# A fused attention and feed-forward kernel: first block's records cut short, output weights loaded and clamped apart, tables from the counts' low words, a new written order

## The chip, the cores and the metric

The kernel runs on one core of a Trainium2 chip. The metric is the device time in microseconds of one execution. Three runs of the kernel before gave 719.63, 720.25 and 720.26 us; their median is 720.25.

## The reference

Attention with a local window, a few global keys and a bias that grows with distance, on q, k, v of 4 batches, 8 heads, 768 positions and 64 columns, all float32; n_local is 96 and n_global is 8. Then a gated feed-forward layer on the 3072 tokens of 512 columns, with 1536 inner columns, whose weights are float64 in the input.

```python
scores = scale * q @ k.T + bias            # bias = -slope_h * distance
scores = where(is_global | is_local, scores, -1e9)
a = softmax(scores)                        # is_local: 0 <= rel < n_local
x = (a @ v) as 3072 x 512
out = (sigmoid(x @ w_gate) * (x @ w_val)) @ w_out
```

## The kernel before

**Blocks.** The tokens are worked in seven blocks: blocks 0 to 3 are three tiles of 128 positions, blocks 4 to 6 four tiles. For each block the attention of four pairs of heads gives x, in a high and a low part (`xh`, `xl`). Then twelve feed-forward steps f, one for each 128 inner columns, multiply x with the gate and value weights of f (`half_in`, L775 for block 0's first step and L787 for the others, into `ps_g` and `ps_u`) and the product with the output weights of f (`ff_out`, L859, into `ps_o`). The gate matmuls of f are three for each of four slices: low weights by high x, high weights by low x, high by high.

**Weights.** The weights come as float64. The kernel makes float32 from them by integer work on the halves of the words, once for each f (twelve blocks; `weights[f]` is 128 x 1536 float64: 1024 columns for gate and value, 512 of output weights). `conv_load` (L176) loads all 1536 columns into one tile `raw` (two buffers). Then come pieces, each one instruction, named by a letter: `B` and `b` (ACT, L194 and L198) take bits of the low words for the 1024 and the 512 columns; `N` and `P` (DVE, L218 and L223) clamp the high half-words in two steps into `neg`; `A` and `a` (DVE, L234 and L236) add them; `H` (ACT, L249) makes the high part `w1h` and `L` (DVE, L182) the low part `w1l`. For f in 2, 4, 6, 8, 10 the clamps of the 1024 columns are done on ACT instead (`Q`, `R`, L209 and L214, and `D` on DVE), and `N` and `P` take the 512 columns only. For the other seven `N` and `P` take 1536 columns.

**The order.** Two strings of words, OPENING and WALK, set the order of every engine's instructions up to the end of block 0: `hold` chains each instruction to the one before on its engine (PE, DVE, ACT, POOL and SP, the queue that issues the DMAs). In OPENING, `S01` is the scores of pair 0, tile 1 (PE, L436), `D01` their reduction with the bias table to a minimum (DVE, L453), `E01` the exponentials with their sums (ACT, L473), `T01` the transposes (PE, L490), `C01` their copy (DVE L499 or ACT L501), `I0` adds and inverts the sums (L506, L508), `R0` spreads the inverses (PE, L516) and `J0` copies them (ACT, L528), `V0` multiplies with the values (PE, L727), `X0` scales, `H0` and `L0` split x, `F0` begins block 0's first feed-forward step, `q`, `v` and `w` load a pair's record, its values and a weight block, `z` and `t` make the bias tables, `k3` is three filler matmuls on zeros (L111), and `c1N` is piece N of weight block 1. In WALK, `G2`, `U2` and `O2` are the gate, value and output matmuls of step 2, `P2` the gate's function (ACT, L798), which frees `ps_g`, `M2` the product (DVE, L807), and `S`, `D`, `E`, `N`, `T`, `C`, `V` the attention of block 1 (L561, L569, L583, L605, L618, L623, L727). From block 1's feed-forward on, a table and a scheduler set the order.

**Records.** `qk` holds for each block and pair the queries, two counts (n_local and n_global as 64-bit words) and the keys by slots: 96 old positions, then for each tile 8 global and 128 own positions, 892 columns in all. The first record is loaded in three transfers, whose first brings the counts, the first tile's queries and its keys. Tile 0 of block 0 uses neither old nor global positions. The counts go through two instructions (L98, L99: low word and sign, then both words) to `nf`, from which the tables and a later check of their range are made.

Of the kernel before, what the change touches and what calls it, by code (L numbers as in the profile page):

```python
# [19 lines left out]
P = 128  # L20
TB = 3
# [11 lines left out]
def attn_moe_kernel(ctx, tc, qT, kT, v, qk, vv, qk4, vv4, weights, out, B, H, S, D):  # L33
# [58 lines left out]
    Q0 = QW - P  # L92
    both = wraw.tile([P, QKW], F32, name="qk", bufs=QB)
# [27 lines left out]
    def build_tables():  # L121

        nl, ng = nf[:, 0:1], nf[:, 1:2]
# [68 lines left out]
    def piece_bits(c):  # L192
        c["bits"] = bits = wraw.tile([P, NW1], I32, name="bits")
        ins = nc.scalar.activation(bits, c["low"][:, 0:NW1], AF.Copy, scale=2.0 ** -13)  # L194
        hold("ACT", behind(ins, last_exp))

    def piece_bits2(c):
        ins = nc.scalar.activation(w2f[c["f"]], c["low"][:, NW1:], AF.Copy, scale=2.0 ** -13)  # L198
        hold("ACT", behind(ins, last_exp))

    def neg_of(c):
        if "neg" not in c:
            c["neg"] = wraw.tile([P, NW], I16, name="neg")
        return c["neg"], NW1 if c["relu"] else 0

    def piece_relu_neg(c):
        if c["relu"]:
            neg, a = neg_of(c)
            hold("ACT", nc.scalar.activation(neg[:, :a], c["high"][:, :a], AF.Relu, scale=-8.0, bias=-8.0 * 14336.0))  # L209

    def piece_relu_top(c):
        if c["relu"]:
            c["top"] = top = wraw.tile([P, NW1], I16, name="top")
            hold("ACT", nc.scalar.activation(top, c["high"][:, :NW1], AF.Relu, scale=8.0, bias=-8.0 * 14336.0))  # L214

# [35 lines left out]
    def piece_low(c):  # L251
# [6 lines left out]
        L=piece_low, Q=piece_relu_neg, R=piece_relu_top,  # L258
    )

    def pieces(j, names):
# [3 lines left out]
        if "loaded" not in c:  # L265
            conv_load(j)
# [53 lines left out]
    def load_step(bi, s):  # L320
# [4 lines left out]
        if bi == 0 and s > 1:  # L325
            qr, kr = (w2f[NF - 1 - 2 * (s - 2) - j].bitcast(F32) for j in range(2))
            hold("SP", nc.sync.dma_start(kr[:, 0:KW], qk[i, :, QW:]))
# [984 lines left out]
```

## Time and profile before

| what | value |
|---|---|
| median of 3 runs | 720.25 us |
| the profiled execution | 720.3 us |
| its span, first to last instruction | 718.5 us |
| PE busy in the span | 709.9 us |
| DVE, ACT, POOL busy | 462.1, 404.4, 180.5 us |
| TensorE's granted clock | 1.0 of full speed throughout |

The span is what the views of the trace cover; 1.8 us of the execution lie around it. A busy time counts an instruction from its start to its modelled end, so PE's busy time holds matmuls that overlap. The first 32 us hold block 0's attention (the opening), and up to about 112 us lie block 0's feed-forward and block 1's attention (the walk).

### The profile page before, as it was taken

How to read it: one execution, taken by the hardware profiler on the slowest of the kernel's cores; microseconds unless marked ns; L12 is line 12 of the kernel's file. 1: busy time of each engine (PE TensorE's matmuls, PEld its weight loads, DVE VectorE, ACT ScalarE, POOL GpSimd, SP SyncE). 2: the span in 40 equal slices, each digit the busy share in tenths (PEclk: the TensorE clock that was granted, in tenths of full speed). 3: DMA queues.
4: the chain of work that ended last, by engine and by line, in shares of the span. 5: the costliest groups of instructions: out<-in, count | busy, mean ns of one | idle time of the engine just before them, and what ended most of it. 6: DMA issues, size and time to landing. Idle time of an engine off the chain costs nothing.

```text
span 718.5 us, 11830 instructions
## 1 busy us (share of the span) xinstructions
PE 709.9 (99%) x4102; PEld 613.0 (85%) x4102; DVE 462.1 (64%) x1237; ACT 404.4 (56%) x956; POOL 180.5 (25%) x177
## 2 busy tenths in 40 slices
PE   8999999999999999999999999999999999999997
PEld 6777789899999999999998888888888888888885
DVE  7989885578867855676876876667677583111112
ACT  7987886565656645665665655455655453322222
POOL 7200012323323322333232223232222121112111
PEclk9999999999999999999999999999999999999999
DMA  8856632635435442353625423324724311100001
GB/s 331 310 204 246 235 110 66 147 62 130 90 89 123 97 95 59 89 136 78 142 64 146 116 69 86 89 56 81 188 58 92 96 39 30 59 0 1 0 1 61
DMA packets 106815, 74.95 MB, mean 104 GB/s; under 512 B 73984, under 2 KB 96896, under 8 KB 105216
## 3 DMA queue, kind: packets, MB, share of 16 engines
q1 hardware_dynamic: 106752, 74.16, 38.6%
q8 instruction: 33, 0.54, 0.3%
q14 instruction: 30, 0.25, 0.1%
HBM read 50.54 MB, written 6.29 MB: 79 GB/s over the span
## 4 chain that ended last, share of the span: by engine, by line
PE 89%; DVE 5%; DMA 2%; ACT 2%; issue 1%; SPq 0%; DVEq 0%
PE ps_u L787 26%; PE ps_g L787 26%; PE ps_o L859 22%; PE ps_s L651 4%; PE ps_t L859 3%; DMA raw<-in_weights 2%; PE ps_v L727 2%; PE ps_s L727 1%; PE ps_t L727 1%; DVE neg L218 1%; DVE neg L223 1%; PE ps_o L890 1%; PE ps_v L561 1%; DVE work L453 1%; PE ps_t L618 1%
## 5 line engine op out<-in xcount | busy, mean ns | idle before, releaser
L182 POOL TENSOR_TENSOR w2l<-w2f,w2h 128x512 fp32r<-128x512 f32 x76 | 103.4, 1360 | 331.4 <-ACT w2h L273 319.2
L787 PE MATMUL ps_g<-xh,w1l 128*128 128x384 f32 (+1 forms) x332 | 121.3, 365 | 0.3 <-ACT work L798 0.2
L787 PE MATMUL ps_u<-xh,w1l 128*128 128x384 f32 (+1 forms) x332 | 120.4, 363 | 0.4 <-DVE work L807 0.4
L787 PE MATMUL ps_g<-xh,w1h 128*128 128x384 f32 (+1 forms) x332 | 119.3, 359 | 0.0
L787 PE MATMUL ps_g<-xl,w1h 128*128 128x384 f32 (+1 forms) x332 | 119.2, 359 | 0.0
L787 PE MATMUL ps_u<-xh,w1h 128*128 128x384 f32 (+1 forms) x332 | 119.2, 359 | 0.0
L787 PE MATMUL ps_u<-xl,w1h 128*128 128x384 f32 (+1 forms) x332 | 119.1, 359 | 0.0
L182 POOL TENSOR_TENSOR qs<-hh,qs 128x256 fp32r<-128x256 f32 x72 | 58.4, 812 | 182.6 <-ACT qs L373 182.2
L807 DVE SCALAR_TENSOR_TENSOR work<-work,ps_u 128x384 f32<-128x384 f32 (+1 forms) x77 | 47.0, 610 | 81.5 <-PE ps_u L787 79.1
L859 PE MATMUL ps_o<-w2l,hh 128*128 128x512 f32 x225 | 88.6, 394 | 0.0
L859 PE MATMUL ps_o<-w2h,hh 128*128 128x512 f32 x225 | 87.7, 390 | 0.0
L583 ACT ACTIVATE work<-work,nms 128x232 f32<-128x232 f32 (+1 forms) x168 | 78.1, 467 | 11.7 <-DVE nms L569 11.6
L859 PE MATMUL ps_o<-w2h,hl 128*128 128x512 f32 x225 | 84.1, 391 | 0.0
L818 ACT ACTIVATE hh<-work 128x384 fp32r<-128x384 f32 (+1 forms) x77 | 43.9, 570 | 63.1 <-DVE work L807 61.1
L182 DVE TENSOR_TENSOR hl<-work,hh 128x384 fp32r<-128x384 f32 (+1 forms) x76 | 50.3, 662 | 40.9 <-PE ps_t L859 27.2
L373 ACT ACTIVATE qs<-hh 128x256 fp32r<-128x256 f32 x72 | 30.0, 417 | 79.4 <-issue 52.5
L569 DVE CUSTOM_DVE_ANT_0 work<-ps_s,tab 128x232 f32<-128x232 f32 x132 | 47.8, 395 | 39.7 <-PE ps_s L651 39.0
L787 PEld LDWEIGHTS ps_g<-xh,w1l 128*128 128x128 f32 x332 | 62.4, 188 | 8.9 <-issue 1.5
L787 PEld LDWEIGHTS ps_u<-xh,w1l 128*128 128x128 f32 x332 | 62.4, 188 | 8.2 <-DVE work L807 0.9
L273 ACT ACTIVATE w2h<-w2f 128x512 fp32r<-128x512 f32 x76 | 47.7, 627 | 38.2 <-PE ps_t L859 21.7
L798 ACT ACTIVATE work<-ps_g 128x384 f32<-128x384 f32 (+1 forms) x84 | 44.2, 526 | 43.7 <-PE ps_g L787 42.6
L787 PEld LDWEIGHTS ps_g<-xl,w1h 128*128 128x128 f32 x332 | 62.5, 188 | 6.6 <-issue 0.2
(193 smaller groups left out, 1288.0 us busy)
## 6 DMA issues: line engine op xcount, KB each, us to landing
raw<-in_weights SPq DMA_DIRECT2D x12, 1536.0 KB, 6.6
vp<-in_vv SPq DMA_DIRECT2D x28, 384.0 KB, 4.1
hh<-in_qk SPq DMA_DIRECT2D x144, 64.0 KB, 2.4
out<-ost SPq DMA_DIRECT2D x21, 256.0 KB, 3.1
kr<-in_qk SPq DMA_DIRECT2D x8, 320.0 KB, 3.2
qk<-in_qk SPq DMA_DIRECT2D x5, 446.0 KB, 7.3
kr<-in_qk SPq DMA_DIRECT2D x8, 252.0 KB, 2.7
hl<-in_vv SPq DMA_DIRECT2D x12, 128.0 KB, 3.1
```

Source lines behind the costliest of these rows:

```text
L182: return eng.tensor_tensor(out, a, b, op=ALU.subtract)
L273: ins = hold("ACT", nc.scalar.activation(hi, w, AF.Copy))
L373: ins = hold("ACT", nc.scalar.activation(qs[:, :, 0], qr, AF.Copy))
L569: ins = nc.vector.tensor_tensor_reduce(sb[:, j, :w], ps[:, :w], (tabs0 if zero else tabs)[2 * s + j], -SCALE, 3.0e38, op0=ALU.add, op1=ALU ...
L583: ins = nc.scalar.activation(sb[:, j, :w], sb[:, j, :w], AF.Exp, scale=-1.0, bias=nm, accum_out=sm[:, j:j + 1])
L651: ins = nc.tensor.matmul(ps[j][:, :w], qs[:, j, hl], st["ks"][:, j, k0:k0 + w], start=(hl == 1), stop=(hl == 0),)
L727: ins = nc.tensor.matmul(av[j * D:(j + 1) * D, t * P:(t + 1) * P], vt[t][:k, j * D:(j + 1) * D], st["pT"][t][:k, m * j + c], start=(c == 0 ...
L787: ins = nc.tensor.matmul(ps[:, :n], wt[f][:, i, c], xt[c], start=(k == 0), stop=(k == 3 * NC - 1))
L798: last_gate[:] = [hold("ACT", nc.scalar.activation(a[:, :n], ps[:, :n], AF.Tanh, scale=0.5))]
L807: hold("DVE", nc.vector.scalar_tensor_tensor(h[:, :n], a[:, :n], 1.0, ps[:, :n], op0=ALU.add, op1=ALU.mult))
L818: hold("ACT", nc.scalar.activation(hh[:, :n], a[:, :n], AF.Copy))
L859: ins = nc.tensor.matmul(outs[bi][t], ht[:, t * P:(t + 1) * P], wt, start=(f == 0 and k == 0), stop=(f == NF - 1 and k == len(parts) - 1),)
```

## The change

Four things are done. The first block's records (`qk0`, a new input) leave out the 104 columns of old and global keys that tile 0 never reads, 788 columns for 892, and its first 128 columns of values stay behind. The first record comes in two transfers, 260 and 528 columns, and the counts stand at its front. The output weights of a block are loaded apart (`o`, tile `rawo`, two buffers, 512 columns of float64, 512 KB) and clamped apart (`n`, `p`, tile `neg2`), so `N` and `P` are 1024 columns wide for seven blocks and gone for five, while `n` and `p` are 512 wide for all twelve. The tables are made from the counts' low words, one copy (`near`); the two instructions that give `nf` come later in the order (word `n`). The strings OPENING and WALK are written anew, with two fillers (`k2`) for three.

```diff
-    for part in (slice(Q0 - CNT, QW + WIN), slice(0, Q0 - CNT), slice(QW + WIN, QKW)):
-        hold("SP", nc.sync.dma_start(both[:, part], qk[0, :, part]))
-    words = both[:, Q0 - CNT:Q0].bitcast(I32).rearrange("p (w h) -> p w h", h=2)
-    wf = cpool.tile([P, 2], F32, name="wf")
-    nc.vector.scalar_tensor_tensor(wf, words[:, :, 0], 0.0, words[:, :, 1], op0=ALU.is_lt, op1=ALU.add)
-    nc.vector.scalar_tensor_tensor(nf, wf, 2.0 ** 32, words[:, :, 0], op0=ALU.mult, op1=ALU.add)
+    for part in (slice(0, CNT + 2 * P), slice(CNT + 2 * P, QK0)):
+        hold("SP", nc.sync.dma_start(both[:, part], qk0[0, :, part]))
+    words = both[:, 0:CNT].bitcast(I32).rearrange("p (w h) -> p w h", h=2)
+    near = cpool.tile([P, 2], F32, name="near")
+    nc.vector.tensor_copy(near, words[:, :, 0])
+
+    def counts():
+        wf = cpool.tile([P, 2], F32, name="wf")
+        hold("DVE", nc.vector.scalar_tensor_tensor(wf, words[:, :, 0], 0.0, words[:, :, 1], op0=ALU.is_lt, op1=ALU.add))
+        hold("DVE", nc.vector.scalar_tensor_tensor(nf, wf, 2.0 ** 32, words[:, :, 0], op0=ALU.mult, op1=ALU.add))
...
-        nl, ng = nf[:, 0:1], nf[:, 1:2]
+        nl, ng = near[:, 0:1], near[:, 1:2]
...
-        raw = wraw.tile([P, 4 * NW + 4], I16, name="raw", bufs=2)
-        hold("SP", nc.sync.dma_start(raw[:, 1:1 + 4 * NW], weights[j].bitcast(I16)))
+        c["low"], c["high"] = load_part(j, "raw", 0, NW1)
...
+    def conv_load2(j):
+        c["low2"], c["high2"] = load_part(j, "rawo", NW1, NW)
...
+    def load_part(j, name, a, b):
+        n = b - a
+        raw = wraw.tile([P, 4 * n + 4], I16, name=name, bufs=2)
+        hold("SP", nc.sync.dma_start(raw[:, 1:1 + 4 * n], weights[j, :, a:b].bitcast(I16)))
...
     def piece_neg(c):
-        neg, a = neg_of(c)
-        ins = nc.vector.tensor_scalar(neg[:, a:], c["high"][:, a:], -18432.0, -14336.0, op0=ALU.max, op1=ALU.min)
-        hold("DVE", behind(ins, last_min))
+        if not c["relu"]:
+            c["neg"] = wraw.tile([P, NW1], I16, name="neg")
+            clamp_low(c["neg"], c["high"])
...
+    def piece_neg2(c):
+        c["neg2"] = wraw.tile([P, DM], I16, name="neg2")
+        clamp_low(c["neg2"], c["high2"])
+
+    def piece_top2(c):
+        clamp_high(c["neg2"], c["high2"])
...
-        hold("SP", nc.sync.dma_start(vp.rearrange("p t c x -> p (t c x)"), vv[bi * NPAIR + s]))
+        cols = slice(P if bi == 0 else 0, TB * 2 * P)
+        hold("SP", nc.sync.dma_start(vp.rearrange("p t c x -> p (t c x)")[:, cols], vv[bi * NPAIR + s, :, cols]))
...
     OPENING = (
-        "S00 q1 z2 k3 D00 z3 S01 z1 E00 S02 D01 E01 T00 S10 S11 D02 t1 w0 T01 E02 v0 T02 t3 S12 C00 D10 "
+        "z2 z1 S00 k2 q1 D00 S01 S02 S10 E00 t1 w0 D01 D02 D10 n t2 E01 o0 T00 E02 S11 S12 v0 t3 C00 T01 I0 "
...
     WALK = (
-        "c2R P0 c2b q1 q0 S0 c2N w3 c2B D0 c2Q E0 G1 c2P M0 c2a c2D P1 c2A v1 N0 v0 S1 U1 D1 O0 c2H E1 M1 "
+        "c2R q0 c2n c2b o3 P0 c2Q c2B M0 c2p S0 D0 G1 E0 c2a w3 c2D c2A q1 o4 N0 S1 c2H D1 c3n U1 c3N c3p E1 "
...
```

How the order moves is shown at three places. The first is ACT in the opening, from the exponentials of pair 0 on (L473 before, L500 in the change: exponentials; L501 and L528: copies of the transposes; L198 and L214: the conversion of the output weights' low words; L528 and L555: the copy of the inverses). Before:

```order
L473 ACTIVATE work,sums<-work,nms 128x232 x4
L501 COPY pT<-ps_o_242 128x512
L198 ACTIVATE w2f_154<-raw 128x512
L501 COPY pT<-ps_t 128x512
L473 ACTIVATE work,sums<-work,nms 128x128 x2
L473 ACTIVATE work,sums<-work,nms 128x232 x4
L528 COPY hl<-ps_o_280 128x384
L473 ACTIVATE work,sums<-work,nms 128x128 x2
```

In the change:

```order
L500 ACTIVATE work,sums<-work,nms 128x232 x4
L500 ACTIVATE work,sums<-work,nms 128x128 x2
L528 COPY pT<-ps_o_259 128x512
L528 COPY pT<-ps_t 128x512
L500 ACTIVATE work,sums<-work,nms 128x232 x2
L555 COPY hl<-ps_o_283 128x384
L214 ACTIVATE w2f_152<-rawo 128x512
L500 ACTIVATE work,sums<-work,nms 128x232 x2
```

The conversion that reads the loaded output weights stood between the two copies of pair 0's transposes; it now stands behind both copies, four exponentials and the copy of the inverses.

The second is SP in the walk (L176 and L193: weights; L334 and L360: records of block 1; L392 and L419: values). Before, from the third weight block on:

```order
L176 DMA raw<-in_weights 128x6144
L334 DMA qk<-in_qk 128x892 x2
L176 DMA raw<-in_weights 128x6144
L392 DMA vp<-in_vv 128x768 x2
L176 DMA raw<-in_weights 128x6144 x4
L334 DMA qk<-in_qk 128x892
L176 DMA raw<-in_weights 128x6144 x2
```

In the change, from the same block's gate weights on:

```order
L193 DMA raw<-in_weights 128x4096
L193 DMA rawo<-in_weights 128x2048
L360 DMA qk<-in_qk 128x892
L193 DMA rawo<-in_weights 128x2048
L193 DMA raw<-in_weights 128x4096
L360 DMA qk<-in_qk 128x892
L193 DMA rawo<-in_weights 128x2048
L193 DMA raw<-in_weights 128x4096
L419 DMA vp<-in_vv 128x768 x2
L193 DMA rawo<-in_weights 128x2048 x2
L193 DMA raw<-in_weights 128x4096 x3
L193 DMA rawo<-in_weights 128x2048
```

Each weight block is two transfers, and the output weights of blocks 5 and 6 stand next to each other ahead of the gate weights of block 5; a transfer that waits for its buffer holds back all that stand behind it.

The third is DVE in the walk ahead of the low half of block 2 (L182 `w1l_144` before, L198 `w1l_142` in the change; L218 and L228: first clamp, L232: second clamp; L569 and L596: reduction; L605 and L632: inverse; L807 and L834: product). Before:

```order
L234 TENSOR_TENSOR bits<-neg,bits 128x1024
L605 RECIPROCAL rc<-sm 128x2
L569 ISA work,nms<-ps_s,tab_113 128x232
L569 ISA nms 128x1
L569 ISA work,nms<-ps_v,tab_114 128x232
L569 ISA nms 128x1
L807 SCALAR_TENSOR_TENSOR hh<-work,ps_u 128x384
L218 TENSOR_SCALAR neg<-raw 128x1536
L182 TENSOR_TENSOR w1l_144<-bits,w1h_132 128x1024
```

In the change:

```order
L256 TENSOR_TENSOR bits<-neg,bits 128x1024
L632 RECIPROCAL rc<-sm 128x2
L596 ISA work,nms<-ps_s,tab_111 128x232
L596 ISA nms 128x1
L596 ISA work,nms<-ps_v,tab_112 128x232
L596 ISA nms 128x1
L228 TENSOR_SCALAR neg_643<-rawo 128x512
L228 TENSOR_SCALAR neg<-raw 128x1024
L232 SCALAR_TENSOR_TENSOR neg_643<-rawo,neg_643 128x512
L198 TENSOR_TENSOR w1l_142<-bits,w1h_130 128x1024
```

One clamp of 1536 columns and a product stood between the reduction and the low half; three clamps stand there now (512, 1024 and 512 columns, of block 3), and the product comes behind it.

## Rows read from the trace of the kernel before

**Rows 1.** The page, part 1: busy us, share of the span, instructions
```profile
PE 709.9 (99%) x4102; PEld 613.0 (85%) x4102; DVE 462.1 (64%) x1237; ACT 404.4 (56%) x956; POOL 180.5 (25%) x177
```

**Rows 2.** Windows: stretch, us, busy us by engine, clock, DMA share, GB/s
```profile
6.50:32.20 25.70, 24.00 (x238) 18.12 (x234) 23.82 (x71) 23.29 (x69) 14.55 (x16) 1.00 0.89 340
```

**Rows 3.** Waits of PE, whole span: us in total, times, longest us
```profile
PE ps_v L727 <- ACT pT L501: 0.8, 1, 0.8
PE ps_t L490 <- ACT work L473: 0.5, 1, 0.5
...
PE ps_t L618 <- ACT pT L623: 0.3, 1, 0.3
```

**Rows 4.** Timeline of the opening: start us, us, engine line operation [idle before]
```profile
3.32 0.16 DVE L98 SCALAR_TENSOR_TENSOR wf<-qk 128x2 f32<-128x2 int32 x1 [1.01 <-DMA qk<-in_qk]
...
3.71 0.34 DVE L150 TENSOR_SCALAR pT<-pT,nf 128x232 f32<-128x232 f32 x1
...
4.62 1.52 PE L111 MATMUL ps_v<-zeros 128*128 128x128 f32 x6
...
6.78 0.40 DVE L453 CUSTOM_DVE_ANT_0 work<-ps_u,tab 128x232 f32<-128x232 f32 x1 [0.67 <-PE ps_u L436]
...
12.08 1.32 PE L727 MATMUL ps_v<-pT,vp 104*64 104x128 f32 x20 [0.79 <-ACT pT L501]
```

**Rows 5.** Timeline of SP; DMA view of that issue: KB, us to landing
```profile
3.17 0.43 SPq L392 DMA_DIRECT2D vp<-in_vv  x1
...
vp<-in_vv SPq DMA_DIRECT2D x1, 384.0 KB, 8.7
```

**Rows 6.** The same two views, two issues that follow each other
```profile
28.22 0.33 SPq L176 DMA_DIRECT2D raw<-in_weights  x1
28.66 0.51 SPq L392 DMA_DIRECT2D vp<-in_vv  x1
...
raw<-in_weights SPq DMA_DIRECT2D x1, 1536.0 KB, 6.6
...
vp<-in_vv SPq DMA_DIRECT2D x1, 384.0 KB, 7.2
```

**Rows 7.** Waits of DVE from 6.5 to 32.2 us
```profile
DVE sums L506 <- ACT work L473: 0.8, 2, 0.4
...
DVE neg L218 <- DMA raw<-in_weights: 0.5, 1, 0.5
```

**Rows 8.** Groups of DVE by shape, 0 to 112 us: busy us, mean ns
```profile
L223 DVE SCALAR_TENSOR_TENSOR neg<-raw,neg 128x1536 int16<-128x1536 int16 x7 | 12.2, 1746 | 0.0
...
L218 DVE TENSOR_SCALAR neg<-raw 128x1536 int16<-128x1536 int16 x7 | 7.8, 1120 | 0.5 <-DMA raw<-in_weights 0.5
...
L223 DVE SCALAR_TENSOR_TENSOR neg<-raw,neg 128x512 int16<-128x512 int16 x5 | 3.4, 688 | 0.0
...
L218 DVE TENSOR_SCALAR neg<-raw 128x512 int16<-128x512 int16 x5 | 2.1, 422 | 0.1
```

**Rows 9.** Timeline: low halves of blocks 1 and 2, and their matmuls
```profile
30.91 1.21 DVE L182 TENSOR_TENSOR w1l<-bits,w1h 128x1024 fp32r<-128x1024 f32 x1
...
32.71 0.44 PE L787 MATMUL ps_g<-xh,w1l 128*128 128x384 f32 x1
...
39.36 1.22 DVE L182 TENSOR_TENSOR w1l<-bits,w1h 128x1024 fp32r<-128x1024 f32 x1
...
41.50 0.42 PE L787 MATMUL ps_g<-xh,w1l 128*128 128x384 f32 x1
```

**Rows 10.** Timeline: clamps of blocks 4 and 5, low half of 5, its matmul
```profile
49.66 0.69 DVE L223 SCALAR_TENSOR_TENSOR neg<-raw,neg 128x512 int16<-128x512 int16 x1
...
53.29 0.96 DVE L218 TENSOR_SCALAR neg<-raw 128x1536 int16<-128x1536 int16 x1
...
64.08 1.22 DVE L182 TENSOR_TENSOR w1l<-bits,w1h 128x1024 fp32r<-128x1024 f32 x1
...
66.88 0.42 PE L787 MATMUL ps_g<-xh,w1l 128*128 128x384 f32 x1
```

More of the change, by code (lines that the diff above doesn't have):

```diff
@@ L32, in attn_moe_kernel @@
 @with_exitstack
-def attn_moe_kernel(ctx, tc, qT, kT, v, qk, vv, qk4, vv4, weights, out, B, H, S, D):
+def attn_moe_kernel(ctx, tc, qT, kT, v, qk, vv, qk4, vv4, qk0, weights, out, B, H, S, D):
     nc = tc.nc
@@ L324, in load_step @@
         i = bi * NPAIR + s
[L325 to L334 removed]
+        if bi == 0:
+            if s > 1:
+                qr, kr = (w2f[NF - 1 - 2 * (s - 2) - j].bitcast(F32) for j in range(2))
+                hold("SP", nc.sync.dma_start(kr[:, 0:K0W], qk0[s, :, NB:NB + K0W]))
+                hold("SP", nc.sync.dma_start(qr[:, 0:NB], qk0[s, :, 0:NB]))
+            elif s:
+                qr = wraw.tile([P, QKW], F32, name="qk", bufs=QB)
+                hold("SP", nc.sync.dma_start(qr[:, 0:QK0], qk0[s]))
+                kr = qr[:, NB:]
+            else:
+                qr, kr = both, both[:, CNT + P:]
+            at = [t * P for t in range(TB)] if s else [CNT, CNT + P + K0W, CNT + 2 * P + K0W]
+            st["q"] = [qr[:, a:a + P] for a in at]
+        elif bi <= PAIR:
+            rec = wraw.tile([P, QKW], F32, name="qk", bufs=QB)
+            hold("SP", nc.sync.dma_start(rec, qk[i]))
             qr, kr = rec, rec[:, QW:]
@@ L430, in scores0 @@
         st = steps[0, s]
-        zero, w, skip = first(t)
+        _, w, skip = first(t)
         ps = [bank("ps_s", "ps_g", "ps_u", "ps_o1") for _ in range(2)]
-        k0 = t * SLOT + skip
+        k0 = t * SLOT + skip - OLD
         for j in (1, 0):
@@ L1253, in _records, with _first_records @@
     return qk.reshape(-1, P, qk.shape[-1]), vv.reshape(-1, P, TB * 2 * P)
+def _first_records(qT, kT, counts, H, D):
+    import numpy as _np
+    pairs, n = H // 2, TB * P
+    keys = n + (TB - 1) * GLOB
+    rec = _np.zeros((pairs, P, CNT + n + keys), _np.float32)
+    q, k = (x[:H * D, :n].reshape(pairs, P, n) for x in (qT, kT))
+    for s in range(pairs):
+        a = n if s else CNT + P
+        for t in range(TB):
+            lo = a + t * SLOT
+            rec[s, :, lo:lo + P] = k[s, :, t * P:(t + 1) * P]
+            if t:
+                rec[s, :, lo - GLOB:lo] = k[s, :, :GLOB]
+        if s:
+            rec[s, :, 0:n] = q[s]
+        else:
+            rec[s, :, 0:CNT].view(_np.int32)[...] = counts.view(_np.int32)
+            rec[s, :, CNT:a] = q[s, :, 0:P]
+            rec[s, :, a + keys:] = q[s, :, P:]
+    return rec
 def _wide_records(qT, kT, v, B, H, S, D):
@@ L1300 @@
     laid["qk4"], laid["vv4"] = _wide_records(laid["qT"], laid["kT"], laid["v"], B, H, S, D)
-    laid = {name: laid[name] for name in ("qT", "kT", "v", "qk", "vv", "qk4", "vv4", "weights")}
+    laid["qk0"] = _first_records(laid["qT"], laid["kT"], counts, H, D)
+    laid = {name: laid[name] for name in ("qT", "kT", "v", "qk", "vv", "qk4", "vv4", "qk0", "weights")}
     nc = _bacc.Bacc("TRN2", target_bir_lowering=False, num_devices=1, dynamic_dma_scratch_size=1024)
```

60 lines of the change are left out of this document (27 added, 33 removed), and 27 rows, old and new, of tables (OPENING, WALK).

## The prediction

> **What bounds the kernel.** I read the page first: TensorE (PE) is busy 709.9 of the span's 718.5 us [rows 1]. The windows say where anything else counts. From 6.5 to 32.2 us, the opening, PE is busy 24.00 of 25.70 us, and VectorE (DVE) 23.82 and ScalarE (ACT) 23.29, so three engines are full at once; the DMA engines are at 0.89 of their time and move 340 GB/s [rows 2]. Then the waits by engine: in the opening PE waits 0.8 us for an ACT copy and 0.5 for ACT's exponentials, and in the walk, up to 112 us, once 0.3 for an ACT copy [rows 3]. The reader is to see that the change edits stretches in which PE has 1.6 us of named waits, plus the filler in front of them, so a gain ends near 2 us whatever is moved. After 112 us no order is changed; what PE waits there I leave as it is.
>
> The sum is made against the profiled execution, 720.3 us (span 718.5 and 1.8 around it); the median of the runs is 720.25, so it carries over.
>
> **Tables and the filler.** The tables' first operation starts at 3.71, and two operations on the counts stand before it, the first at 3.32 [rows 4]. One copy of the low words takes the place of both: at two equal operations, 0.2 us earlier. It is not on PE's path. The first wide reduction (6.78) waits 0.67 for the scores S01, and on PE these stand right behind three filler matmuls, which began at 4.62 and took 1.52 us: 0.5 for one [rows 4]. One filler less: S01, and with it DVE's chain, starts **0.5 earlier**, near 5.6. Its cover is the second transfer of the first record, which has to land by 5.6; if it doesn't, the 0.5 shrinks. The two operations on the counts come back later among the reductions: 3.71 - 3.32 = **0.4 more** on DVE in the opening.
>
> **Clamps apart.** The second clamp takes 1746 ns on 1536 columns and 688 on 512, so 529 per 512 and 159 fixed; on 1024 it is 1217, and both halves together cost 0.16 more. The first: 1120 and 422, so 349 per 512 and 73 fixed, 0.07 more [rows 8]. That is 0.23 for each weight block whose clamps are all on DVE, seven of twelve: two in the opening (**0.5**), five in the walk (1.2 over some 80 us, which I cost at nothing; its cover is looked at below).
>
> **Columns left behind.** 52 KB less per record and 64 KB less of values, four of each, is 464 KB, at 340 GB/s [rows 2] 1.4 us of queue time over the whole opening. It counts only where a wait ends on a landing. DVE waits 0.5 for the first weights [rows 7], and ACT for the same landing in front of the copy that PE waits for. For that copy the order is what helps: ACT's copies C01 and C02 now stand ahead of the conversion of the output weights, so the **0.8** goes [rows 3]. What is late next is the first values: issued at 3.2, they land 8.7 later, at 11.9 [rows 5], while PE now starts on them at 12.1 [rows 4]. 168 KB less stand in front, 0.5 us, so PE gets 0.7 of the 0.8.
>
> **The opening's sum.** On PE: 0.5 + 0.7 and perhaps some of the second wait, 1.2 to 1.7. But the opening ends when DVE ends it: the low half of weight block 1 runs from 30.91 to 32.12, and PE needs it at 32.71 [rows 9], so PE can gain at most 0.6 more than DVE. DVE: -0.5 (start) + 0.4 (counts) + 0.5 (clamps) = +0.4 with all its waits kept; the waits are 0.8 for the sums and 0.5 for the weights [rows 7], so -0.9 with none kept. In the new order two more reductions stand ahead of the first clamp, which covers the 0.5, and the block-1 clamp ahead of the last sums, which covers one 0.4; I take -0.5 for DVE. PE, with up to 0.6 of slack behind it, is then 0.5 to 1.1 ahead; I take **-0.8**, ends +0.4 and -1.7.
>
> **The walk.** The transposes that wait 0.3 for a copy [rows 3] now stand behind the next gate and scores, and the copy stands earlier on ACT: **-0.3**. Against it, the low half of block 2 ends at 39.36 + 1.22 = 40.58 and PE starts on it at 41.50, 0.9 later [rows 9]. In the new order three clamps stand in front of it (422 + 771 + 688 ns, by the same rows) where one of 1120 stood: +0.8. The cover is nearly used up, and I cost it at nothing because DVE arrives 0.5 earlier. The gate P1, too, is moved on ACT behind a conversion and an exponential, and it frees the bank that the same matmuls write.
>
> Sum: -0.8 - 0.3 = -1.1, so **719.2 us**. About 0.2%, 1.4 us, is what a measurement of this kernel can tell from no change, so this forecast stands inside "same", near its edge.
>
> **Rule against the change.** A transfer issued 0.4 us behind a whole weight block (28.66 and 28.22) landed 7.2 after its issue against 6.6, so 1.0 later, for 384 KB [rows 6]: near 390 GB/s, with no fixed time of its own. The Trainium skill, "DMA: Bandwidth & Descriptors", section Bandwidth, says to batch transfers to 1 MiB or more to come to three quarters of the peak; the output weights now travel alone in 512 KB. By that rule twelve transfers would each lose, and the rival below would gain weight; by the row they lose nothing while others queue behind them.
>
> **Rivals.**
> *All waits go* (chance 0.33). If DVE's waits all vanish, PE takes the whole of its own: filler 0.5, waits 0.8 + 0.5 + 0.3: -2.1, and 718.2; the interval is 717.7 to 718.8. For it: both engines' waits lie early, and the order was open to be written around them. Against it: DVE's 0.9 of added work in a stretch where it is 93% busy.
>
> *Weights queue behind weights* (0.11, slower). SP issues in order. The gate weights of block 5 now stand behind the output weights of block 6, which take the buffer of block 4's and so wait for its clamp. That clamp ended at 49.66 + 0.69 = 50.35; the two transfers, 1536 KB together, take 6.6 [rows 6] and land at 56.9, where DVE read block 5 at 53.29. That is 3.6 late; the low half of block 5, 64.08 to 65.30, has 1.6 until PE wants it at 66.88 [rows 10]. So 2.0 are lost: 722.3 if the opening gives nothing. It decides from the point where DVE reaches that clamp more than 1.6 us before the landing. Against it: in the new order block 4's low half (1.2) and the two clamps of block 5's output weights (1.1) come first, which leaves 1.3 of the 3.6.
>
> *Each transfer pays for itself* (0.02, slower). If the output weights' transfers cost a fixed time after all, the first values land later than 11.9: a whole microsecond late, and as much again at the second pair, is 722.3. Rows 6 speak against it.
>
> *Nothing moves* (0.15, in "same"). DVE keeps its waits, +0.4 there, covered by PE's 0.6 of slack, and the walk's 0.3 is lost again at block 2: 720.3.
>
> **Numbers.** The forecast's own case has 0.39, 718.9 to 720.2. Faster by over 0.2%: 0.35, the first rival and a little of the forecast's edge. Same: 0.52. Slower: 0.13. The range has to reach into the first rival and past "nothing moves": 717.8 to 721.0 leaves out the slow cases and a few hundredths below.
>
> **What would show it.** In the changed profile: S01 near 5.6; the first values on PE near 11.5 with no 0.8 wait for an ACT copy; the low half of block 1 ending near 31.6 and the walk starting 0.5 to 1 us earlier; no transposes waiting in the walk; block 2's matmuls with little or no wait for its low half. The prediction is wrong if DVE shows new waits for weights near 53, if PE waits at block 2 for its gate's bank or its low half, or if stretches after 112 us, whose order is the same, differ by more than a few tenths.

## The result and the profile after

The changed kernel takes **724.35 us** (median of six runs, 721.70 to 726.55), the kernel before 720.24 beside it (six runs, 719.63 to 720.63): ratio 1.0058, 95% interval 1.0042 to 1.0074. It is 4.1 us slower where I had forecast 1.1 faster, and the time lies above my range (717.8 to 721.0). The runs also lie 4.9 us apart, against 1.0 for before. The execution that was profiled took 725.86 us, 5.6 more than that of before.

The page, part 1, of the changed kernel; PE is busy 1.7 us longer than in [rows 1], in a span 5.6 us longer:

```profile
PE 711.6 (98%) x4100; PEld 613.4 (85%) x4100; DVE 466.1 (64%) x1252; ACT 404.0 (56%) x956; POOL 179.1 (25%) x177
```

The windows of the changed kernel (columns as in [rows 2]), then those of before for the stretches that had not been shown:

```profile
6.50:32.20 25.70, 21.93 (x226) 17.00 (x223) 24.45 (x75) 22.62 (x65) 12.48 (x15) 1.00 0.78 283
32.20:112.00 79.80, 78.94 (x440) 60.44 (x439) 71.11 (x142) 64.57 (x134) 3.37 (x2) 1.00 0.57 208
112.00:200.00 88.00, 85.63 (x517) 79.36 (x517) 60.05 (x176) 52.99 (x136) 27.30 (x26) 1.00 0.44 98
```

```profile
32.20:112.00 79.80, 79.48 (x444) 61.55 (x445) 70.41 (x137) 66.44 (x138) 3.08 (x2) 1.00 0.54 197
112.00:200.00 88.00, 87.19 (x526) 80.54 (x525) 61.69 (x182) 54.15 (x137) 28.10 (x27) 1.00 0.46 102
```

In the opening PE does 21.93 us of work where it did 24.00, and DVE 24.45 for 23.82: the engine that was to come 0.5 us earlier is the fuller one. From 112 us on, where I had said that nothing moves, PE does 1.6 us less. The waits of PE in the changed kernel, whole span:

```profile
PE ps_g L802 <- DVE w1l L198: 1.2, 1, 1.2
PE ps_o L886 <- POOL w2l L198: 1.1, 2, 0.8
...
PE ps_u L814 <- DVE hh L834: 0.9, 1, 0.9
PE ps_v L754 <- ACT pT L528: 0.7, 1, 0.7
PE ps_s L678 <- POOL qs L198: 0.7, 1, 0.7
...
PE ps_v L754 <- DMA vp<-in_vv: 0.4, 1, 0.4
```

The three waits of [rows 3] are gone from their places, and others have come: the low half of weight block 0 (L198, 1.2), a product in the walk (L834, 0.9), a copy of a later pair (L528, 0.7, at 22.7 us), low parts that POOL makes late (1.1 and 0.7, at 128 to 142 us), the first values' landing (0.4). PE's timeline has the first values at 12.00, where I had said 11.5 and the kernel before has 12.08 [rows 4]:

```profile
12.00 1.21 PE L754 MATMUL ps_v<-pT,vp 104*64 104x128 f32 x18 [0.43 <-DMA vp<-in_vv]
```

The waits are not the whole: the lag against the kernel before (the same matmul's start in both traces) is 1.35 us at the first walk matmul, G1 (34.06 against 32.71 [rows 9]), and 3.89 at 400 us, but 5.5 at the end, with no wait between. The chain of waits has a gate group near 400 us and the last output matmuls (start us, us); first of the kernel before, then of the changed one:

```profile
397.18 2.74 PE ps_g L787 x12
...
708.49 4.15 PE ps_o L890 x18
```

```profile
401.07 2.76 PE ps_g L814 x12
...
714.02 4.17 PE ps_o L917 x18
```

Between them lie 311.31 us before and 312.95 now, for the same matmuls in the same order: 1.6 us.

### The profile page after: what moved, and what is told of

Its sections match the earlier page's. It is cut to its first block, busy times and chain, and to the rows that moved or that the text cites. A ratio compares the mean times of both kernels' runs of the same rounds, so it can differ in the third digit from the quotient of the medians.

```text
span 724.1 us, 11856 instructions
## 1 busy us (share of the span) xinstructions
PE 711.6 (98%) x4100; PEld 613.4 (85%) x4100; DVE 466.1 (64%) x1252; ACT 404.0 (56%) x956; POOL 179.1 (25%) x177
## 4 chain that ended last, share of the span: by engine, by line
PE 84%; DMA 6%; DVE 3%; ACT 3%; issue 3%; POOL 1%; SPq 1%; ACTq 0%; POOLq 0%; DVEq 0%
PE ps_u L814 25%; PE ps_g L814 24%; PE ps_o L886 22%; PE ps_s L678 4%; PE ps_t L886 3%; DMA raw<-in_weights 3%; PE ps_v L754 2%; DMA hh<-in_qk 1%; PE ps_s L754 1%; DMA vp<-in_vv 1%; PE ps_t L754 1%; POOL w2l L198 1%; PE ps_o L917 1%; DVE neg L232 1%; ACT work L610 0%
## 5 line engine op out<-in xcount | busy, mean ns | idle before, releaser
L198 POOL TENSOR_TENSOR w2l<-w2f,w2h 128x512 fp32r<-128x512 f32 x76 | 103.3, 1360 | 332.4 <-ACT w2h L293 312.7
L198 POOL TENSOR_TENSOR qs<-hh,qs 128x256 fp32r<-128x256 f32 x72 | 58.6, 814 | 185.6 <-ACT qs L399 185.6
L834 DVE SCALAR_TENSOR_TENSOR work<-work,ps_u 128x384 f32<-128x384 f32 (+1 forms) x77 | 47.0, 610 | 80.8 <-PE ps_u L814 77.2
L198 DVE TENSOR_TENSOR hl<-work,hh 128x384 fp32r<-128x384 f32 (+1 forms) x76 | 49.4, 650 | 43.7 <-PE ps_t L886 27.6
L596 DVE CUSTOM_DVE_ANT_0 work<-ps_s,tab 128x232 f32<-128x232 f32 x132 | 47.7, 394 | 35.0 <-PE ps_s L678 34.6
L814 PEld LDWEIGHTS ps_g<-xh,w1h 128*128 128x128 f32 x332 | 62.4, 188 | 5.8
```

Of the source, the lines that this page charges most:

```text
L198: return eng.tensor_tensor(out, a, b, op=ALU.subtract)
L596: ins = nc.vector.tensor_tensor_reduce(sb[:, j, :w], ps[:, :w], (tabs0 if zero else tabs)[2 * s + j], -SCALE, 3.0e38, op0=ALU.add, op1=ALU ...
L814: ins = nc.tensor.matmul(ps[:, :n], wt[f][:, i, c], xt[c], start=(k == 0), stop=(k == 3 * NC - 1))
L834: hold("DVE", nc.vector.scalar_tensor_tensor(h[:, :n], a[:, :n], 1.0, ps[:, :n], op0=ALU.add, op1=ALU.mult))
```

## The experiments

Fourteen kernels, each timed in five rounds beside the kernel before on the same chip (its medians there 719.67 to 720.26). What they gave, in one table; each is taken up below:

| run | median us | range | ratio | 95% interval |
|---|---|---|---|---|
| place | 723.11 | 720.59 to 725.27 | 1.0044 | 1.0030 to 1.0058 |
| shift | 721.82 | 721.16 to 722.31 | 1.0025 | 1.0014 to 1.0036 |
| shift64 | 722.92 | 721.58 to 724.10 | 1.0036 | 1.0022 to 1.0050 |
| order_only | 725.05 | 722.34 to 727.06 | 1.0079 | 1.0062 to 1.0095 |
| parts_only | 719.77 | 719.23 to 720.73 | 1.0000 | 0.9991 to 1.0009 |
| open_only | 722.15 | 720.36 to 723.96 | 1.0031 | 1.0020 to 1.0043 |
| walk_only | 718.88 | 717.43 to 720.79 | 0.9987 | 0.9978 to 0.9996 |
| tail | 723.40 | 719.77 to 726.72 | 1.0063 | 1.0040 to 1.0086 |
| open_fix | 722.38 | 719.12 to 724.47 | 1.0032 | 1.0017 to 1.0046 |
| open_turn | 720.76 | 720.32 to 723.56 | 1.0014 | 1.0004 to 1.0023 |
| w5_first | 720.06 | 718.62 to 722.82 | 1.0009 | 0.9997 to 1.0021 |
| copy_first | 718.13 | 716.98 to 719.01 | 0.9975 | 0.9966 to 0.9984 |
| three | 719.89 | 719.13 to 722.71 | 1.0005 | 0.9995 to 1.0015 |
| four | 719.26 | 717.94 to 721.49 | 0.9993 | 0.9982 to 1.0003 |

**Addresses.** With `near` there is one small tile of 8 bytes more, which pushes every tile that is allocated after the tables (products, halves, output weights, transposes) 32 bytes on. Three runs: place puts them back in the changed kernel, shift and shift64 move them in the kernel before.

```diff
-    nf = cpool.tile([P, 2], F32, name="nf")
+    nfw = cpool.tile([P, 8], F32, name="nf")
+    nf = nfw[:, 0:2]
...
-        wf = cpool.tile([P, 2], F32, name="wf")
+        wf = nfw[:, 2:4]
```

> The changed kernel, with the two counts' scratch tile (wf) kept inside the tile nf, so that every tile behind the tables stands at the address it has in the kernel before, and not 32 bytes further on; instructions and order are the changed kernel's. In the changed kernel's profile the matmuls of blocks 4 to 6 follow each other at 226 to 237 ns, in that of before at 226 and 227, and its lag grows from 3.9 us at 400 us to 5.6 at the end with no wait of TensorE behind it. Theory (the addresses make the matmuls slower): the intervals are back at 226 and 227, the lag of the end is about 3.8, the median near 722.6 and the runs closer together. Rival (chance of that one execution, or the new order): still 724.4, with 722 to 726.5 over the runs.

```diff
     nms = cpool.tile([P, 2 * (B * NTB * NPAIR)], F32, name="nms")
+    cpool.tile([P, 2], F32, name="pad")
```

> The kernel before with one unused tile of 8 bytes behind the tables, which moves every later tile by 32 bytes, as the change does; not an instruction differs. Theory (addresses): matmuls of blocks 4 to 6 at 228 to 237 ns where another engine works beside them, 1.5 to 2 us lost, near 722. Rival (the order or chance): 720.2 as before.

> The kernel before with two unused tiles of 8 bytes, 64 bytes of address in all, where shift has one and 32. Theory (the kernel's operands lie at offsets that keep TensorE's reads apart from the others', and any step of this size spoils it): 721.5 to 722.3, like shift. Rival (only the odd step of 32 does it, a multiple of 64 is as good as none): 720.0.

The chain of waits of shift, and then of place, at the same two groups:

```profile
397.70 2.76 PE ps_g L788 x12
...
710.48 4.17 PE ps_o L891 x18
```

```profile
401.45 2.74 PE ps_g L815 x12
...
712.29 4.13 PE ps_o L918 x18
```

Between them lie 312.78 us in shift (before: 311.31) and 310.84 in place. So the 1.6 us of the end are the addresses: they come with an unused tile, and go when the tile goes. All sixteen profiles say the same: this stretch takes 312.6 to 313.0 us in the three with moved addresses (the changed kernel, shift, shift64) and 310.8 to 311.3 in the other thirteen, whatever their order. The groups of PE by shape from 620 to 708 us (last columns: busy us, mean ns), of shift and then of place, show where:

```profile
L788 PE MATMUL ps_g<-xl,w1h 128*128 128x512 f32 x44 | 17.3, 392 | 0.0
...
L788 PE MATMUL ps_u<-xl,w1h 128*128 128x512 f32 x41 | 15.9, 389 | 0.0
...
L860 PE MATMUL ps_o<-w2l,hh 128*128 128x512 f32 x33 | 13.0, 394 | 0.0
```

```profile
L815 PE MATMUL ps_g<-xl,w1h 128*128 128x512 f32 x44 | 17.1, 389 | 0.0
...
L815 PE MATMUL ps_u<-xl,w1h 128*128 128x512 f32 x42 | 16.3, 389 | 0.0
...
L887 PE MATMUL ps_o<-w2l,hh 128*128 128x512 f32 x33 | 12.8, 389 | 0.0
```

In these rows gate and output matmuls are 3 to 5 ns longer and the value matmuls not; in the groups left out one of the value groups is 2 ns longer, too, and one of the gate and one of the output groups is not. Counted one by one from 640 to 710 us, 119 of 306 matmuls of the changed kernel start 228 ns or more ahead of the next, and 0 of 309 before. Beside a product, its rounding or its low part (on DVE and ACT) it is 76 of 98, beside other work of ACT and POOL 6 of 74, with nothing beside them 37 of 134. So the writes beside them are not the whole cause, and which accesses meet is open. shift64 is no better than shift, and worse than I gave it (its profile also has the late clock that is taken up below). place's median falls only 1.2 us below the changed kernel's, and its runs still lie 4.7 apart: the spread is not the addresses.

**Parts or order.** order_only has the instructions of before in the changed order, parts_only the changed instructions in the order of before (with place's addresses). In order_only block 5's output weights are put together without their second clamp, which comes behind the addition; the work is the same. The edit of parts_only begins:

```diff
-        "z2 z1 S00 k2 q1 D00 S01 S02 S10 E00 t1 w0 D01 D02 D10 n t2 E01 o0 T00 E02 S11 S12 v0 t3 C00 T01 I0 "
+        "S00 q1 z2 k3 D00 z3 S01 z1 E00 S02 D01 E01 T00 S10 S11 D02 t1 w0 o0 T01 E02 v0 T02 t3 S12 C00 D10 n "
...
```

> The kernel before with the changed kernel's order (both strings), as far as its instructions go: whole weight blocks in one transfer where the gate weights travel, the clamps of a block in one piece, the counts ahead of the tables, the first records whole. Theory (the order loses in the opening 1.3, at 64 us 0.7 and behind the walk, where the scheduler turns queries and output weights round on GpSimd and SyncE, 1.7): 722.5 to 724, with GpSimd's low parts of queries and of output weights waited for at 125 to 145 us. Rival (the separate transfers and clamps lose it): 720 to 721.

> The changed kernel's records, transfers, clamps and tables in the order of before (each output transfer right behind its gate weights, each of the 512-column clamps right behind the 1024-column one, the counts behind the third reduction), with the addresses of before. Theory (the parts cost little or nothing, the order and the addresses lose): 719.5 to 720.8. Rival (each part pays: more clamps on VectorE, smaller transfers, the ring of DMAs full sooner): 722 or more, with waits for weights in the walk.

The parts alone cost nothing (1.0000). place has the same parts and addresses in the new order and is at 1.0044: that is what the order costs. order_only has the order with the old parts and lost more (1.0079) than I gave it, and not by what the changed kernel loses: the waits for POOL that I had expected at 125 to 145 us are not in its profile, and PE stands there for exponentials longer than in any other. Its windows (clock in the third column from the end) have the clock's own part in it:

```profile
PE ps_v L727 <- ACT work L473: 2.0, 1, 2.0
```

```profile
22.00:23.60 1.60, 0.01 (x2) 0.04 (x2) 1.60 (x7) 1.00 (x5) 0.05 (x1) 1.00 0.93 342
...
25.10:28.50 3.40, 3.40 (x16) 3.26 (x14) 3.40 (x2) 2.62 (x5) 1.87 (x1) 0.50 0.35 142
```

PE had stood 2.0 us for exponentials, up to 23.6; the granted clock then fell to 0.50, its lower level of 1.2 GHz, until 28.5.

**Opening or walk.** The two strings apart, on place's addresses:

> The changed kernel with the addresses of before (as in place) and with its new order in the opening alone; the walk has the order of before (each output transfer and its clamps right behind those of its gate weights), and so has all behind it. In the profiles so far the new opening lags by 1.3, 2.2 and 3.3 us at the first wide feed-forward matmuls, and in two of them TensorE waits 1.1 to 1.2 there for the low half of weight block 0. Theory (most of the order's 3.3 us between parts_only, 719.8, and place, 723.1, is lost in the opening): 721.3 to 722.3, and runs apart by 2 us or more. Rival (the walk and the seam behind it lose it): 720.0 to 720.7.

> As open_only, the other way round: the opening in the order of before, the walk in the new one. Theory (the opening loses most, the walk the rest): 720.7 to 721.5, with TensorE waiting 0.5 to 1.2 near 60 to 68 us for a product or a gate. Rival (the walk and the seam): 722 or more.

The opening loses 0.31%, and the new walk, behind the old opening, is 0.13% *faster* than before. Neither the theory (walk loses the rest) nor the rival has this. 0.31 - 0.13 is 0.18, short of place's 0.44 by 0.26, with some 0.2 of uncertainty from the three intervals, so it is likely that the two together lose something that neither has alone. The tail of the walk is not it:

```diff
-        "D11 X2 c11a E11 c11L W9 P10 Y2 T9 C9 Z a0 G11 M10 b0 N11 T10 C10 H10 L10 O9 P11 T11 C11 W10 U11 M11 "
-        "H11 W11 a1 V3 X3 L11 Y3 O10"
+        "D11 X2 c11a E11 c11L W9 P10 Y2 T9 C9 G11 N11 Z T10 a0 C10 O9 T11 M10 b0 H10 U11 P11 C11 W10 M11 a1 "
+        "L10 O10 H11 V3 W11 X3 L11 Y3"
```

> The changed kernel with the addresses of before, its last 32 words of the walk put back into the order of before; with them the scheduler orders all that follows as in the kernel before. In the changed kernel's profile TensorE waits 0.3, 0.7 and 0.8 at 128 to 142 us for low parts that GpSimd makes late, ScalarE standing ahead of them in front of landings of queries; in place there is no such wait, with TensorE 2.5 us later. Theory (the new tail is exposed to these landings and costs when the rest comes early): place less 0.3 to 1, 722.1 to 722.8, and no wait at 122 to 144 us. Rival (it never counts, the lag comes from before it): 723.1 as place.

A miss: 723.4, the rival, with runs as far apart as the changed kernel's (719.8 to 726.7). POOL's late low parts cost PE 1.8 us in the one execution of the changed kernel that was profiled (after its waits above); in place, tail and walk_only no such wait stands.

**One word of the walk.** In the changed kernel, DVE's timeline (start us, us):

```profile
55.59 0.69 DVE L232 SCALAR_TENSOR_TENSOR neg<-rawo,neg 128x512 int16<-128x512 int16 x1
56.20 1.22 DVE L198 TENSOR_TENSOR w1l<-bits,w1h 128x1024 fp32r<-128x1024 f32 x1
58.90 0.69 DVE L228 TENSOR_SCALAR neg<-raw 128x1024 int16<-128x1024 int16 x1 [1.48 <-DMA raw<-in_weights]
```

and SP's and PE's:

```profile
51.28 0.33 SPq L193 DMA_DIRECT2D rawo<-in_weights  x1
51.65 1.50 SPq L193 DMA_DIRECT2D raw<-in_weights  x2
...
64.23 0.45 PE L814 MATMUL ps_u<-xh,w1l 128*128 128x384 f32 x1 [0.86 <-DVE hh L834]
```

That is the rival of my prediction, by the way it had named: block 5's gate weights go out right behind block 6's output weights, DVE has done the low half and the two clamps that I had counted as cover, stands 1.48 us, and its product comes 0.86 late for PE. In place DVE stands 2.56 us, the transfer taking 8.29 from issue to landing; in walk_only the same order has it land at 55.04 with DVE there at 55.07.

```diff
-        "O0 w4 c2L P1 S2 c4R M1 c3B c3P T0 G2 c3b D2 c3A E2 v0 C0 S3 v1 N1 P2 U2 o5 o6 c3a c3H D3 w5 N2 O1 S4 "
+        "O0 w4 c2L P1 S2 c4R M1 c3B c3P T0 G2 c3b D2 c3A E2 v0 C0 S3 v1 N1 P2 U2 o5 w5 c3a c3H D3 o6 N2 O1 S4 "
```

> place (the changed kernel with the addresses of before) with two words of the walk exchanged: the gate weights of block 5 are issued ahead of the output weights of block 6 and no longer behind them. In the changed kernel's profile VectorE stands 1.5 us for their landing at 58.9, in place 2.6 us at 62.2, and TensorE then 0.9 and 1.2 us for a product near 64 to 67 us; in walk_only they land at 55.04 and VectorE comes at 55.07. Theory (SyncE issues in order, and block 5 waits for a buffer that the other transfer waits for; it costs 0.9 to 1.9 where the opening comes late): VectorE's wait goes, 721.9 to 722.4. Rival (VectorE is the bound there and the wait only gives it rest): 723.1.

With two words exchanged place falls from 1.0044 to 1.0009, more than expected, and DVE no longer waits for these weights; its timeline:

```profile
55.93 1.22 DVE L199 TENSOR_TENSOR w1l<-bits,w1h 128x1024 fp32r<-128x1024 f32 x1
57.07 0.69 DVE L229 TENSOR_SCALAR neg<-raw 128x1024 int16<-128x1024 int16 x1
```

This is what opening and walk lose together: behind the new opening these weights come too late for the new walk. Eight of its twelve runs are at 718.6 to 720.7, four at 722.0 to 722.8.

**The opening.** Two kernels, two reasons. open_fix takes a pile-up apart; DVE of the changed kernel, then POOL (two low parts of x from 23.13 to 25.56):

```profile
23.14 1.55 DVE L232 SCALAR_TENSOR_TENSOR neg<-rawo,neg 128x512 int16<-128x512 int16 x1
24.61 2.03 DVE L198 TENSOR_TENSOR w1l<-bits,w1h 128x1024 fp32r<-128x1024 f32 x1
...
23.13 2.43 POOL L198 TENSOR_TENSOR xl<-hh,xh 128x384 fp32r<-128x384 f32 x2
```

Elsewhere these two of DVE take 0.69 and 1.22, as the rows at 55.59 and 56.20 above show.

```diff
-        "D21 E20 v1 z3 c0B v2 X0 T11 C11 S22 S30 T20 D22 H0 c0a I1 E22 E21 V1 R1 T21 w1 c0A C20 D30 T22 I2 "
-        "S31 S32 J1 R2 E30 v3 c0H c1N D31 C22 w2 o2 c1n C21 X1 V2 H1 E31 D32 T30 E32 L0 T32 c1p T31 C30 c0L "
+        "D21 E20 v1 z3 c0B v2 X0 T11 C11 S22 S30 T20 D22 H0 c0a I1 E22 E21 V1 R1 T21 w1 c0A C20 D30 T22 I2 L0 "
+        "S31 S32 J1 R2 E30 v3 c0H c1N D31 C22 w2 o2 c1n C21 X1 V2 H1 E31 D32 c0L T30 E32 T32 c1p T31 C30 C32 "
```

> The changed kernel with the addresses of before; in the opening the low half of weight block 0 (c0L, VectorE) is put right behind the second wide reduction of pair 3, ahead of a clamp, and GpSimd's first low part of x (L0) ahead of the second high part, as before. In the profiles VectorE took 1.55 and 2.03 us for a clamp and that low half while GpSimd made two low parts beside them, where 0.69 and 1.2 are usual. Theory (this pile-up is what the new opening loses): TensorE's wait of 1.1 to 1.2 for that low half goes, 722.0. Rival (TensorE only waits elsewhere, all three engines being full): 723.1 as place.

The wait for the low half goes, as expected, but the gain is 1.0044 to 1.0032, inside both intervals: unclear by itself. The pile-up has only moved: in open_fix's profile the low half takes 1.23, the clamp, now behind it, 1.50, and POOL's low part 1.99. What the runs show instead is two groups, 719.1 to 721.6 and 723.2 to 724.5, six and six. So has open_only (720.4 to 721.4 and 722.9 to 724.0). open_turn goes after them:

```diff
-        "z2 z1 S00 k2 q1 D00 S01 S02 S10 E00 t1 w0 D01 D02 D10 n t2 E01 o0 T00 E02 S11 S12 v0 t3 C00 T01 I0 "
+        "z2 z1 S00 k2 q1 D00 S01 S02 E00 t1 w0 D01 T00 S10 D02 D10 n t2 E01 o0 T01 E02 S11 S12 v0 t3 C00 I0 "
```

> open_only with the transposes T00 and T01 put back ahead of the scores S10 and S11 on TensorE, where the order of before has them; nothing else. In the profiles TensorE's clock comes up to its upper level at 4.3 to 5.9 us in some executions; in others it stays at the lower one, where the 232-column scores follow at 0.38 us and not 0.19, until 10.2 and 10.5 us in the opening of before (shift, parts_only) and until 13.4 and 13.8 in the new one (open_fix, place), in which TensorE had stood 0.06 us for the first wide reduction at 7.7. The twelve runs of open_only fall into two groups, 720.4 to 721.4 and 722.9 to 724.0, those of open_fix too. Theory (the upper group is the late clock, and the new TensorE order makes it 3 us later than the old): no runs above 722, median 720.5 to 721.2. Rival (the groups come from something else, a transfer or VectorE): still about half of the runs at 722.9 to 724.

Ten of eleven runs are now at 720.3 to 721.7; the upper group is gone but for one run, as the theory had it. The lower level shows in PE's timelines by the distance of the 232-column scores: first the changed kernel, then place, where the same scores are twice as far apart.

```profile
6.00 0.36 PE L463 MATMUL ps_u<-qk 64*128 64x232 f32 x1
6.19 0.36 PE L463 MATMUL ps_g<-qk 64*128 64x232 f32 x1
...
6.39 0.35 PE L463 MATMUL ps_g<-qk 64*128 64x232 f32 x1
```

```profile
6.33 0.59 PE L464 MATMUL ps_u<-qk 64*128 64x232 f32 x1
6.71 0.59 PE L464 MATMUL ps_g<-qk 64*128 64x232 f32 x1
...
7.09 0.59 PE L464 MATMUL ps_g<-qk 64*128 64x232 f32 x1
```

The clock column is 1.00 in both, since its record only begins when the clock comes up: at 5.6 us in the changed kernel's profile, at 13.8 in place's. (So the "1.0 of full speed throughout" of the kernel before holds only from 5.9 us on.) The profiled executions that came up at 4 to 6 us lie in the lower groups of their kernels (open_only 720.43, w5_first 719.51), the two at 13.4 and 13.8 among the upper runs (open_fix 723.19, place 724.18). In the order of before the clock came up late, too, at 10.2 to 10.6 (shift, parts_only, shift64), at less cost: G1 starts at 33.3 to 33.5 there, for 32.71, and at 35.0 and 36.0 in the two of the new opening, for 32.7 to 34.1 in those with an early clock. shift and parts_only have no two groups; shift64's six runs lie 2.5 us apart, which I can't assign.

The clock is not all of the spread. The changed kernel's 725.86 us has an early clock: its time is the 1.35 of the opening, the product's wait, POOL's 1.8 and the addresses' 1.6. And early profiles with one and the same opening (tail, w5_first, the changed kernel) reach G1 at 32.74, 33.16 and 34.06; their first values landed at 10.46, 11.29 and 11.87, and PE started on them at 10.83, 11.43 and 12.00. So part of the spread is likely that of the landings.

**Together.**

> The changed kernel with three causes undone at once and nothing else: the addresses of before (place), the gate weights of block 5 issued ahead of block 6's output weights (w5_first), the transposes T00 and T01 ahead of the scores S10 and S11 (open_turn). Theory (these three are the loss, each by itself): the upper group of w5_first (722.0 to 722.8, the late clock) is gone, 719.2 to 719.8, and below or at the kernel before. Rival (the causes stand in for one another, or a fourth is left): 720.5 or more.

> three, and the two words of open_fix: the low half of block 0 right behind the reduction, GpSimd's first low part earlier. Theory (the pile-up of VectorE and GpSimd holds TensorE 1.1 us at the first feed-forward matmuls, of which what is left after the next waits is 0.4 to 0.8): 718.6 to 719.2. Rival (all three engines are full there and TensorE waits 0.7 to 1.0 at the next place instead): 719.5 as three.

With the three causes undone the loss is gone (1.0005, its interval holds 1), though not below before, and w5_first alone had most of that (1.0009): the turned order, worth 0.17% between open_only and open_turn, adds nothing here that can be told. Two runs of eleven are still at 722 and above, so the theory that the upper group goes is not borne out. four gains 0.12% more, as large as in open_fix, and again inside the intervals; the pile-up is likely worth 0.6 us, and isn't settled.

The profiles, one execution of each kernel, can be cut into three stretches: up to G1, from G1 to the gate group near 400 us, and from there to the last output matmuls (all in us). They put each cause into its own stretch:

| profile | clock up | G1 at | to the gate group | to the last outputs |
|---|---|---|---|---|
| before | 5.9 | 32.71 | 364.5 | 311.3 |
| parts_only | 10.5 | 33.47 | 364.2 | 310.8 |
| shift | 10.2 | 33.28 | 364.4 | 312.8 |
| walk_only | 4.9 | 33.04 | 362.7 | 310.9 |
| open_only | 4.8 | 33.59 | 364.2 | 310.8 |
| tail | 4.3 | 32.74 | 364.4 | 310.8 |
| place | 13.8 | 36.00 | 365.5 | 310.8 |
| w5_first | 3.9 | 33.16 | 363.5 | 311.1 |
| three | 4.4 | 33.16 | 363.5 | 310.9 |
| the changed kernel | 5.6 | 34.06 | 367.0 | 313.0 |

In the middle stretch the new walk is some 1.5 us shorter than the old one where block 5's weights are in time (walk_only), and not shorter, or longer, where they are late behind the new opening (tail, place); the exchange of two words (w5_first, three) makes it 0.9 shorter than tail's and 2.0 shorter than place's. The changed kernel has POOL's 1.8 there as well.

**A version that beats both.** walk_only with the one move of the opening on which my largest term rested: the copy of pair 0's transposes ahead of the conversion of block 0's output weights.

```diff
-        "I0 C01 c0b D11 C02 c0N c0n R0 E10 V0 E11 D12 E12 q2 c0P c0p T10 J0 S20 T12 v1 C10 q3 D20 t2 X0 T11 "
+        "I0 C01 D11 C02 c0b c0N c0n R0 E10 V0 E11 D12 E12 q2 c0P c0p T10 J0 S20 T12 v1 C10 q3 D20 t2 X0 T11 "
```

> walk_only (the opening of before, the new walk, the addresses of before) with one word moved in the opening: ScalarE's conversion of block 0's output weights goes behind the copy of pair 0's last transposes. It is the move for which I had forecast 0.7 us at the first values; in walk_only's profile TensorE waits 1.4 there for that copy. Theory (it is worth what I forecast, and the full VectorE behind it gives part back): 718.1 to 718.5, and TensorE's wait at 12.2 us for the copy gone. Rival (VectorE and ScalarE are full behind it, nothing is left at the first feed-forward matmuls): 718.9 as walk_only.

718.13 us, 0.25% faster than before, where the changed kernel is 0.58% slower. PE's waits from 6 to 112 us, of walk_only and then of copy_first:

```profile
PE ps_v L755 <- ACT pT L529: 1.4, 1, 1.4
PE ps_t L518 <- ACT work L501: 0.5, 1, 0.5
```

```profile
PE ps_v L755 <- DMA vp<-in_vv: 0.8, 1, 0.8
PE ps_t L518 <- ACT work L501: 0.5, 1, 0.5
```

The copy's 1.4 went, 0.8 for the values' landing came in its place, and 0.75 us is the difference of the medians, 0.12% by the ratios, whose intervals overlap: the size is likely, not settled.

## Why the prediction was wrong

**What held.** The clamps, transfers and cut records were costed at next to nothing, and parts_only is 1.0000. By the rule of the Trainium skill, "DMA: Bandwidth & Descriptors", section Bandwidth, the smaller transfers would lose. parts_only shows no loss, in a kernel whose PE waits for none of them. The first wide reduction came earlier, at 6.41 for 6.78 [rows 4]. Block 2's low half was reached without a wait. The 0.7 for the first values is right in size where the copy is moved alone, in copy_first (0.75). In the changed kernel's profile it is missing: I had counted on a landing 0.5 us earlier than 11.9 for the columns left behind, and the values landed at 11.87. The walk gains, 0.9 in walk_only where I gave it 0.3; its profile is 1.7 us shorter than that of before from G1 to 400 us, and the waits of PE that have gone there, the copy's 0.3 and a gate's 0.2, make 0.5 of that. So the sign and the mechanism are right, and where the larger part comes from no run shows.

**The opening's sum failed.** The -0.8 for PE in the opening is, by open_only against parts_only, +2.2 by the ratios. The step that failed is "I take -0.5 for DVE", which set a time for each of DVE's instructions from rows where nothing ran beside them. Two of them met POOL's low parts and took 0.86 and 0.81 us longer; the low half of block 0 ended at 26.64, and PE waited 1.2 for it where I had PE ahead by 0.8. That wait is shown; what it costs in the end is not settled (0.12% by open_fix, by four the same, inside the intervals). And the sum has no clock. I had read a granted clock of 1.0 and taken the filler as 0.5 us of waste. In about half of open_only's runs the time is 2.6 us longer, the distance of its two groups, and a clock that comes up late is the likely cause: G1 starts 1.4 and 2.4 us later than open_only's in the two profiles that have it (35.0 and 36.0 for 33.6). That the scores ahead of the transposes and the wait behind them make it late is argued from open_turn (0.17% better) and not shown by itself.

**The rival I gave 0.11 came true.** "Weights queue behind weights" has its place, its wait and its order of size in the profile. What I set against it, 2.3 us of other work for DVE, was there, too. I had mis-sized the transfer: 6.6 us for two, where three were under way and the gate weights took 7.2 and 8.3, and I had taken a walk that starts on time.

**Nothing after 112 us: that failed twice.** I had written that no order is changed there. The order there is the scheduler's and not the words': POOL and SP take queries and output weights in another order behind the new walk, which cost 1.8 in one execution and 0 to 0.3 in others. And no order has to move for an address to move: 1.8 us by shift, the surest part of the loss, from a tile of 8 bytes that I had read as one copy less.

The terms, by the ratios: the opening costs 0.31% and the walk gives back 0.13%; place has 0.26% more than these two, which is what late weights of block 5 can account for, as w5_first takes 0.35% back; the addresses are 0.25% by shift and 0.14% from place to the changed kernel. That makes 0.58 to 0.69% where 0.58% was measured, each term being uncertain by 0.1 or more.

## What to carry to other kernels

Compare where the tiles lie, not only the instructions: a new small tile ahead of others can cost more than what it saves, and an unused one shows it. Where three engines are full, judge a written order by the runs' spread too, since an order without slack turns every late clock or landing into time. Try the parts of a rewrite apart; here the parts were free, the new opening was a loss, the new walk a gain, and one word of it a loss again behind a late opening.

## What the runs showed of the hardware that I had not expected

- The pace of TensorE's matmuls depends on where tiles lie: they follow each other at 226 and 227 ns in the kernel before, and 119 of 306 at 228 to 237 in the changed one; an unused tile that moves others by 32 bytes does the same and costs 0.25%, two of them 0.36%. The Trainium skill, "SBUF — State Buffer", section "SBUF: two separate sides", says that PE never waits on anyone there. The measurement does not fit that, and decides, though what PE waits for was not found: of those with a product, its rounding or its low part beside them (VectorE, ScalarE) 76 of 98 are the long ones, but so are 37 of the 134 with nothing beside them.
- The clock came up from its lower level (1.2 GHz) to the upper (2.4 GHz) at 3.9 to 5.9 us in eleven profiles and at 10.2 to 13.8 in five, and one opening can do both: 5.9 and 10.2 in the order of before (before, shift), 3.9 and 13.8 in the new one (w5_first, place). PE stood 0.06 us at 7.7 in the two latest. That this gap kept it down is argued from open_turn, which removes the wait and turns the order at once; three, with the same turn, still has two runs of eleven at 722 and above.
- A clamp of 0.69 us took 1.55, a low half of 1.22 took 2.03, with a GpSimd subtraction beside each. The same section of the Trainium skill, "SBUF: two separate sides" in "SBUF — State Buffer", has VectorE (with two inputs in SBUF) and GpSimd share a pair of ports that the one that starts first holds for its whole instruction. The rows fit: in the changed kernel GpSimd starts first, at 23.13, and takes 1.01 while the clamp, at 23.14, takes 1.55; in tail the clamp starts first, at 21.86, and takes 0.71 while GpSimd, at 21.87, takes 1.56.
- The same 1 MB of weights took 5.7, 7.2 and 8.3 us to land with two others under way (walk_only, the changed kernel, place). Why is open.
